# mm2's seven products in one PSUM bank, pages handed out one by one, a fourth block of mm1 by seven products, and a new order of work

## The chip, the cores and the metric

The kernel runs on one core of one Trainium2 chip. The core has five engines that work side by side: TensorE (PE, whose weight loads the profile lists as PEld), VectorE (DVE), ScalarE (ACT), GpSimd (POOL) and SyncE (SP, which issues most of the DMA transfers). The metric is the device time of one execution in microseconds; the figure for the kernel before is the median of three runs, 296.69 us (296.46 to 296.79).

## The reference

Retention attention without softmax, followed by a feed-forward layer:

```python
# q, k, v: [8 batches, 8 heads, 576 positions, 64], float32
scores = matmul(q, k.T) / 8
gamma  = 1 - 2.0 ** (-5 - head)
D      = where(i >= j, gamma ** (i - j), 0)          # per head
attn   = matmul(scores * D, v)
x      = attn.transpose(0, 2, 1, 3).reshape(4608, 512)
h      = x @ w_in                                    # w_in  [512, 2048]
g      = 0.5 * h * (1 + tanh(c * (h + 0.044715 * h**3)))
out    = g @ w_out                                   # w_out [2048, 512], out float32
```

## The kernel before

Attention is done in units of 128 positions of one batch with all eight heads: four full units and a tail of 64 positions for each of eight batches, 40 units in all. Units 0, 2, 5 and 7 are "wide": they hold 256 positions, and the next unit number belongs to them. Within a unit the scores of a half of 64 positions are computed directly and masked; what came before goes through a running state of decayed k-v products, one for each head. q and v are scaled by powers of the decay when they are cast to 16 bits (`cast_q`, `cast_k`, `cast_v`; L424, L439, L269), q and k are transposed by a DMA (`dma_T`, L483) or on PE (`pe_T`, L493, with `copy_T` reading the result), `attend` (L529 to L574) holds the scores, the k-v products and the outputs, `masked` (L691), `state_sum` (L713), `state_decay` (L721) and `state_16` are the steps on DVE, ACT and POOL, and `x_out` (L586 to L599) writes the result into xT.

The feed-forward layer works on nine blocks t of 512 tokens. mm1 (`x @ w_in`) is done in one of two ways. Directly: `mm1` (L757) multiplies 128 rows of w_in for each output and `gelu` (L765) reads the bank. Or by seven products instead of eight (Strassen's scheme in Winograd's form): `sum_w` and `sum_x` prepare sums of blocks of w_in and of x, `product_h` (L957) runs product 1 to 7 of a group of four output columns tiles, `part_h` reads partial results out of PSUM, and `gelu_h` (L975) makes the outputs. Blocks 6, 7 and 8 go this way, the others directly. Products 1, 6, 7 and 4 of `product_h` add onto each other in one bank, and `part_h` copies the state between them.

mm2 (`g @ w_out`) is done directly for block 0 and half of block 8 (`mm2`, L783, and `mm2_cols`, L987), and by seven products for the 15 other pairs of 128-token tiles: `sum_b` and `sum_a` prepare sums of w_out and of g, `product` (L860) runs the products into two PSUM banks, and `assemble` reads them: two copies and five sums for each pair. All sums go through `combine` (L817), all plain copies through `copy_on` (L267 on ACT, L269 on DVE or POOL).

PSUM has eight banks: two for mm1 ("h"), two for mm2 ("o"), two for scores and two for attention outputs. `take` hands out the banks of a pool in turn.

Inputs: `load` (L203 to L221) brings q, k and v of a unit by SP into pages of float32. There are 21 pages, in groups of three: unit u uses group u % 7 up to unit 30, and from unit 31 on one of the first three groups, because pages 9 to 20 then hold the sums for mm1's seven products. The weights are loaded and cast to 16 bits by transfers that POOL issues (L238); w_in comes in eight loads, two for each quarter of its columns, and so does w_out. `busy` (L1003) multiplies the identity on PE without use of the result.

The order of the work on every engine is written out as a list of short steps at the head of the file. A step's letter chooses the function and the numbers its arguments. Each engine runs its own steps in the order of the list and waits by semaphores for what it needs. The letters that matter here: L load, I and J loads of w_in and w_out, q k v casts, D and t transposes, B attend, a o z the state, m mask, x output, N and F mm1 and gelu for half a block's tokens (two tiles of w_in's columns in one bank), s U A l f the seven products of mm1, H T W V those of mm2, S the stores, K busy work.

Of the kernel before, what the change touches and what calls it, by code (L numbers as in the profile page):

```python
# [17 lines left out]
L,0,1 Z,1,v L,0,0 I,2,g L,0,2 L,2,1 L,2,0 Z,2,g q,0 k,0,g I,7,g K,4 K,4 K,4 K,3 K,4 t,0,q,h L,2,2  # L18
L,4,1 c t,0,k,h I,1,g v,0,v X,0 y,0,k,v I,0,g I,3,g a,0,1 y,0,q,v Z,3,v k,2,g K,4 K,1 Y,0,1 t,2,k,o
m,0,1 z,0,1,a I,6,g K,4 Y,0,0 a,1,1 q,2 L,4,0 K,4 t,2,q,h m,0,0 y,2,k,a y,2,q,v I,4,g K,1 R,0 I,5,g  # L20
x,0 Y,2,1 L,5,0 x,1 i,4,v K,3 N,0,2,0 N,0,0,0 g o,1,1 m,2,1 L,5,1 Z,4,g v,2,v F,0,2,0 N,0,12,0 Y,2,0
F,0,0,0 z,1,1,v N,0,4,0 L,5,2 X,2 k,4,g Z,5,v q,4 F,0,12,0 F,0,4,0 t,4,k,o a,2,1 t,4,q,o a,3,1
y,4,q,a N,0,8,0 L,4,2 z,2,1,g L,9,1 N,0,10,0 F,0,8,0 k,5,g m,2,0 L,7,1 R,2 F,0,10,0 y,4,k,v B,4,-1
q,5 x,3 x,2 N,0,14,0 L,7,0 t,5,q,o N,0,0,1 L,7,2 J,1,g F,0,14,0 N,0,6,0 y,5,q,v J,3,g t,5,k,o
F,0,0,1 m,4 j,1,v J,0,g L,9,0 v,5,v J,2,g L,9,2 F,0,6,0 N,0,8,1 L,10,0 N,0,12,1 k,7,v X,5 y,5,k,a
F,0,8,1 z,3,1,g F,0,12,1 v,4,v Y,5,0 a,5,1 m,5,0 a,6,1 N,0,4,1 N,0,6,1 F,0,4,1 q,7 F,0,6,1 t,7,k,o
y,7,k,a N,0,2,1 J,5,g J,4,g N,0,14,1 F,0,2,1 J,6,g L,10,2 B,-1,4 F,0,14,1 x,4 Y,5,1 t,7,q,h y,7,q,a
J,7,g m,5,1 N,0,10,1 v,7,v F,0,10,1 z,5,1,g R,5 x,5 Y,7,0 o,6,1 x,6 O,0,0 O,0,4 q,10,g L,11,1
N,1,4,0 O,0,5 N,1,14,0 F,1,4,0 m,7,0 N,1,2,0 L,12,2 O,0,1 X,7 Y,7,1 F,1,14,0 F,1,2,0 L,15,1 k,9,a
# [12 lines left out]
V,1,0,6,v L,16,0 N,2,10,0 F,2,10,0 k,14,g W,1,1,6 V,1,1,1,v N,2,12,0 z,12,1,v L,16,2 B,13,12 x,12
# [84 lines left out]
def kernel(  # L127
# [38 lines left out]
    def ring(pool, shape, dtype, tag, name, bufs):  # L166
        rings[tag] = n = rings.get(tag, -1) + 1
        return pool.tile(shape, dtype, tag=f"{tag}_{n % bufs}", name=name, bufs=1)

    NR = 7
    pages = const.tile([128, 3 * NR, H, D], F32, name="pages")
    raws = [pages[:, 3 * i : 3 * i + 3] for i in range(NR)]


    LATE = 31

    def raw_of(u):
        return u % NR if u < LATE else (u - LATE) % 3  # L180

    WIDE = (0, 2, NC, NC + 2)

# [888 lines left out]
```

## Time and profile before

| what | value |
|---|---|
| median of three runs | 296.69 us |
| the profiled execution: time, and span of its instructions | 295.65 us, 293.9 us |
| PE busy | 280.3 us (95%), 4064 matmuls |
| DVE, ACT, POOL busy | 216.6, 150.1, 109.6 us |
| DMA | 49.79 MB, mean 169 GB/s |
| granted PE clock | 1.0 in the whole span |

The profile counts an engine as busy from the start of an instruction to its end; matmuls overlap each other, so a busy PE is not a measure of PE at its peak, and the distance between two starts is the better price of one. A line of a group gives the line of the kernel, the engine, the operation, what it writes and reads with the shape, how many there were, the busy time, and the idle time of the engine before them with what ended it. The chain of waits is followed back from the last instruction: at each step to what released it.

### The profile page before, as it was taken

How to read it: one execution, taken by the hardware profiler on the slowest of the kernel's cores; microseconds unless marked ns; L12 is line 12 of the kernel's file. 1: busy time of each engine (PE TensorE's matmuls, PEld its weight loads, DVE VectorE, ACT ScalarE, POOL GpSimd, SP SyncE). 2: the span in 40 equal slices, each digit the busy share in tenths (PEclk: the TensorE clock that was granted, in tenths of full speed). 3: DMA queues.
4: the chain of work that ended last, by engine and by line, in shares of the span. 5: the costliest groups of instructions: out<-in, count | busy, mean ns of one | idle time of the engine just before them, and what ended most of it. 6: DMA issues, size and time to landing. Idle time of an engine off the chain costs nothing.

```text
span 293.9 us, 9639 instructions
## 1 busy us (share of the span) xinstructions
PE 280.3 (95%) x4064; PEld 235.2 (80%) x4064; DVE 216.6 (74%) x447; ACT 150.1 (51%) x289; POOL 109.6 (37%) x168
## 2 busy tenths in 40 slices
PE   3797999999999999999999999999999999999995
PEld 1355886667888888888888888888888788888874
DVE  7686753696865678576678699799889988977740
ACT  2144774334634543554553646546777587665411
POOL 5931910414351084163415544783467123000000
PEclk9999999999999999999999999999999999999999
DMA  7999999997979999989099978899498370002103
GB/s 212 283 236 250 217 220 211 214 179 162 248 142 228 178 186 220 230 206 210 23 235 214 196 166 178 187 204 153 131 195 208 75 205 7 36 8 102 74 25 121
DMA packets 136428, 49.79 MB, mean 169 GB/s; under 512 B 118208, under 2 KB 130880, under 8 KB 136384
## 3 DMA queue, kind: packets, MB, share of 16 engines
q1 hardware_dynamic: 132032, 44.97, 71.3%
q0 software_dynamic: 4352, 4.20, 8.5%
q8 instruction: 32, 0.52, 0.8%
q14 instruction: 12, 0.10, 0.1%
HBM read 36.70 MB, written 9.44 MB: 157 GB/s over the span
## 4 chain that ended last, share of the span: by engine, by line
PE 86%; POOL 5%; DMA 4%; DVE 3%; issue 1%; ACT 0%; POOLq 0%; ACTq 0%
PE bank L860 30%; PE bank L757 27%; PE bank L957 12%; PE bank L783 6%; DMA w_in_sb<-in_moe_w_in_dram 4%; PE sk L553 2%; PE x L529 2%; POOL w_in_sb L238 2%; PE sk L563 1%; PE x L574 1%; PE bank L987 1%; DVE pages L817 1%; POOL wide L269 1%; PE bank L493 1%; PE x L677 1%
## 5 line engine op out<-in xcount | busy, mean ns | idle before, releaser
L757 PE MATMUL bank<-xT,w_in_sb 128*128 128x256 f16 x768 | 94.4, 273 | 2.1 <-DMA w_in_sb<-in_moe_w_in_dram 2.1
L765 ACT ACTIVATE gT<-bank 128x512 f16<-128x512 f32 x96 | 56.7, 598 | 61.5 <-PE bank L757 59.7
L757 PEld LDWEIGHTS <-w_in_sb 128*128 128x128 f16 x768 | 73.8, 98 | 13.7 <-DMA w_in_sb<-in_moe_w_in_dram 2.7
L860 PEld LDWEIGHTS <-ssum 128*128 128x128 f16 x480 | 46.3, 98 | 6.5 <-issue 0.8
L269 POOL CAST sz<-s 64x256 f16<-64x256 f32 x48 | 24.4, 509 | 66.2 <-DVE s L713 45.9
L860 PE MATMUL bank<-tsum,ssum 128*128 128x256 f16 x360 | 46.0, 273 | 0.6 <-DVE ost L817 0.6
L860 PEld LDWEIGHTS <-gT 128*128 128x128 f16 x360 | 34.8, 98 | 4.5 <-issue 0.2
L424 POOL TENSOR_TENSOR qk<-pages,dec 128x512 f16<-128x512 f32 (+1 forms) x20 | 22.2, 1122 | 32.9 <-DMA pages<-in_q_dram 17.2
L860 PE MATMUL bank<-w_out_sb,gT 128*128 128x256 f16 x240 | 31.1, 273 | 0.0
L817 DVE TENSOR_TENSOR ssum<-gT 128x1024 f16<-128x1024 f16 x30 | 23.9, 798 | 3.9 <-ACT gT L765 3.5
L424 POOL TENSOR_TENSOR v<-pages,dec 128x512 f16<-128x512 f32 (+1 forms) x20 | 20.6, 1030 | 15.3 <-DMA pages<-in_v_dram 10.4
L817 DVE TENSOR_TENSOR ost<-u,bank 128x256 f32<-128x256 f32 x45 | 18.1, 416 | 9.5 <-PE bank L860 9.4
L817 DVE TENSOR_TENSOR ssum<-gT,ssum 128x1024 f16<-128x1024 f16 x30 | 23.4, 782 | 0.2
L691 DVE TENSOR_TENSOR ret<-sk,mask 128x512 f16<-128x512 f32 (+1 forms) x32 | 19.8, 618 | 4.3 <-PE sk L563 4.0
L957 PEld LDWEIGHTS <-pages 128*128 128x128 f16 x192 | 18.4, 98 | 2.8 <-issue 0.3
L957 PE MATMUL bank<-pages 128*128 128x256 f16 x144 | 20.3, 273 | 0.3 <-ACT pages L267 0.3
L783 PE MATMUL bank<-w_out_sb,gT 128*128 128x512 f16 x80 | 19.1, 380 | 0.0
L817 DVE TENSOR_TENSOR u<-u,bank 128x256 f32<-128x256 f32 x30 | 12.4, 415 | 8.7 <-PE bank L860 5.0
L713 DVE TENSOR_TENSOR s<-s,sk 128x256 f32<-128x256 f32 x36 | 14.9, 415 | 5.0 <-PE sk L563 4.0
L593 ACT ACTIVATE xT<-x 128x512 f16<-128x512 f32 (+1 forms) x25 | 14.3, 578 | 8.0 <-PE x L574 8.0
L817 DVE TENSOR_TENSOR hc<-hc,bank 128x512 f32<-128x512 f32 x21 | 14.4, 684 | 5.0 <-PE bank L957 2.3
L267 ACT COPY hc<-bank 128x512 f32<-128x512 f32 x19 | 11.1, 585 | 12.5 <-PE bank L957 12.4
(114 smaller groups left out, 425.8 us busy)
## 6 DMA issues: line engine op xcount, KB each, us to landing
out_dram<-ost SPq DMA_DIRECT2D x35, 256.0 KB, 3.4
pages<-in_q_dram SPq DMA_DIRECT2D x32, 256.0 KB, 4.7
pages<-in_v_dram SPq DMA_DIRECT2D x24, 256.0 KB, 4.1
pages<-in_k_dram SPq DMA_DIRECT2D x24, 256.0 KB, 4.3
pages<-in_k_dram SPq DMA_DIRECT2D x4, 512.0 KB, 5.2
pages<-in_v_dram SPq DMA_DIRECT2D x4, 512.0 KB, 6.0
w_in_sb<-in_moe_w_in_dram POOLq DMA_DIRECT2D x8, 256.0 KB, 9.8
w_out_sb<-in_moe_w_out_dram POOLq DMA_DIRECT2D x8, 256.0 KB, 10.6
```

The lines of the kernel that those rows point to most:

```text
L267: nc.scalar.copy(out=o, in_=i)
L269: (nc.vector if eng == "v" else nc.gpsimd).tensor_copy(out=o, in_=i)
L424: eng.tensor_tensor(out=out, in0=s["raw"][:, i, 0:n], in1=dec[:, i // 2, s["j"], 0:n].unsqueeze(2).to_broadcast([128, n, D]), op=ALU.mult,)
L593: nc.scalar.activation(out=xT[:, :, o : o + G * (b - a)].rearrange("c p (h s) -> c p h s", s=G), in_=x[:, a:b].rearrange("c h p s -> c p h ...
L691: nc.vector.tensor_tensor(out=ret[:, :, 0:n], in0=now["two"][:, :, 0, 0:n], in1=mask.unsqueeze(1).unsqueeze(1).to_broadcast([128, 2, n, G] ...
L713: nc.vector.tensor_tensor(out=s32, in0=state[0], in1=kv, op=ALU.add)
L757: nc.tensor.matmul(hps[:, i, :], w_in_sb[:, ct, 128 * (fc + i) : 128 * (fc + i) + 128], xT[:, ct, TB * t % XR + lo : TB * t % XR + hi], st ...
L765: nc.scalar.activation(out=gTs[t][:, fc : fc + TB // (hi - lo), lo:hi], in_=h.pop((t, fc, lo)), func=AF.Gelu_apprx_tanh, bias=0.0, scale=1.0,)
L783: nc.tensor.matmul(ops[t, tcc], gTs[t][:, ft, 128 * tcc : 128 * tcc + 128], w_out_sb[:, ft, :], start=(ft == 0), stop=(ft == NFC - 1),)
L817: (nc.vector if eng == "v" else nc.gpsimd).tensor_tensor(out=out, in0=a, in1=b, op=op)
L860: nc.tensor.matmul(p["ps", bank][:, HN * col : HN * col + HN], a[:, k], b[:, k], start=(k == 0 and i in (1, 6)), stop=(k == HK - 1), skip_ ...
L957: nc.tensor.matmul(p["ps", bank][:, n], w[:, c, 128 * n : 128 * n + 128], x[:, c], start=(n == 0 and c == 0 and i in (1, 2, 5)), stop=(c = ...
```

## The change

Five things change together.

- `product` and `assemble`: products 1, 6, 7 and 4 of a pair now add onto the same half of the first bank, with a copy of the state taken out between them (four copies, one of them straight into the output tile). Products 2, 5 and 3 go into the second bank; three sums read them. The copies can be given to ACT or DVE, the sums are on DVE. A pair had two copies and five sums.
- Pages: `page` and `read` hand out single pages from a list of free ones, the longest free first; a wide load takes two neighbours. From unit 26 on, or once the sums of w_in have begun, only pages 0 to 8 are used.
- mm1 of block 5 is done by seven products too, so four blocks instead of three.
- mm1 of block 0 and block 4 is partly done in other shapes: the new steps M and G do a quarter of the block's tokens for four column tiles in one bank (128 columns for each matmul), or all 512 tokens for one tile.
- The list of steps is made anew: order, and which engine takes each cast and copy. Unit 23 is transposed on PE instead of by DMA, the busy work falls from 36 to 20 matmuls, and the stores and loads stand in other places.

Some further options are added to functions and not used by the list (`sum_a` with 5, `masked` with "h", `state_sum` on POOL).

```diff
-    raws = [pages[:, 3 * i : 3 * i + 3] for i in range(NR)]
-    LATE = 31
-    def raw_of(u):
-        return u % NR if u < LATE else (u - LATE) % 3
+    LATE = 26
+    free = [12, 13, 14] + list(range(12)) + list(range(15, 3 * NR))
+    page_of, sums_on = {}, [False]
+    def page(u, n, width=1):
+        top = 9 if u >= LATE or sums_on[0] else 3 * NR
+        at = {p: i for i, p in enumerate(free) if p < top}
+        p = min(
+            (p for p in at if p + width - 1 in at), key=lambda p: (max(at[p], at[p + width - 1]), p)
+        )
+        for i in range(width):
+            free.remove(p + i)
+        page_of[u, n] = p
+        return p
+    def read(u, n, width=1):
+        free.extend(range(page_of[u, n], page_of[u, n] + width))
...
     def product(t, pr, i):
-        if i in (1, 6):
-            p["ps", 0 if i == 1 else 1] = take("o")
         a, b, bank, col = {
-            1: (blk_a(t, pr, 0, 0), blk_b(0, 0), 0, 0), 2: (blk_a(t, pr, 0, 1), blk_b(1, 0), 0, 0),
-            3: (s[3], blk_b(1, 1), 1, 1), 4: (blk_a(t, pr, 1, 1), tsum[3], 0, 1),
-            5: (s[0], tsum[0], 1, 1), 6: (s[1], tsum[1], 1, 0), 7: (s[2], tsum[2], 0, 1),
+            1: (blk_a(t, pr, 0, 0), blk_b(0, 0), 0, 0), 2: (blk_a(t, pr, 0, 1), blk_b(1, 0), 1, 0),
+            3: (s[3], blk_b(1, 1), 1, 1), 4: (blk_a(t, pr, 1, 1), tsum[3], 0, 0),
+            5: (s[0], tsum[0], 1, 1), 6: (s[1], tsum[1], 0, 0), 7: (s[2], tsum[2], 0, 0),
         }[i]
+        fresh = ("ps", bank) not in p
+        if fresh:
+            p["ps", bank] = take("o")
...
     def assemble(t, pr, i, eng):
-        if i == 0:
-            copy_on(eng, part_of(t, pr, 1), ps(0, 0))
-        elif i == 1:
-            combine(eng, part_of(t, pr, 2), part_of(t, pr, 1), ps(1, 0), ALU.add)
-        elif i == 2:
-            copy_on(eng, block_c(t, pr, 0, 0), ps(0, 0))
-        elif i == 3:
-            combine(eng, part_of(t, pr, 3), part_of(t, pr, 2), ps(0, 1), ALU.add)
-        elif i == 4:
-            combine(eng, block_c(t, pr, 1, 1), part_of(t, pr, 3), ps(1, 1), ALU.add)
-        elif i == 5:
-            combine(eng, block_c(t, pr, 1, 0), part_of(t, pr, 2), ps(0, 1), ALU.add)
-        else:
-            combine(eng, block_c(t, pr, 0, 1), part_of(t, pr, 2), ps(1, 1), ALU.add)
+        if i in (0, 1, 3):
+            copy_on(eng, part_of(t, pr, (1, 2, 0, 3)[i]), ps(0, 0))
+        elif i == 5:
+            copy_on(eng, block_c(t, pr, 1, 0), ps(0, 0))
+        elif i == 2:
+            combine("v", block_c(t, pr, 0, 0), part_of(t, pr, 1), ps(1, 0), ALU.add)
+        elif i == 4:
+            combine("v", block_c(t, pr, 1, 1), part_of(t, pr, 3), ps(1, 1), ALU.add)
+        else:
+            combine("v", block_c(t, pr, 0, 1), part_of(t, pr, 2), ps(1, 1), ALU.add)
```

The head of the list, where the start is decided, before and after:

```diff
-L,0,1 Z,1,v L,0,0 I,2,g L,0,2 L,2,1 L,2,0 Z,2,g q,0 k,0,g I,7,g K,4 K,4 K,4 K,3 K,4 t,0,q,h L,2,2
-L,4,1 c t,0,k,h I,1,g v,0,v X,0 y,0,k,v I,0,g I,3,g a,0,1 y,0,q,v Z,3,v k,2,g K,4 K,1 Y,0,1 t,2,k,o
-m,0,1 z,0,1,a I,6,g K,4 Y,0,0 a,1,1 q,2 L,4,0 K,4 t,2,q,h m,0,0 y,2,k,a y,2,q,v I,4,g K,1 R,0 I,5,g
-x,0 Y,2,1 L,5,0 x,1 i,4,v K,3 N,0,2,0 N,0,0,0 g o,1,1 m,2,1 L,5,1 Z,4,g v,2,v F,0,2,0 N,0,12,0 Y,2,0
+I,1,g g L,4,1 L,2,0 L,0,0 q,2 Z,5,v q,0,g k,4,a L,0,1 L,0,2 k,0,a K,4 K,4 K,4 K,4 K,2 K,1 t,0,q,h
+L,4,0 I,0,g Z,1,v y,0,q,v Z,3,v t,0,k,h t,2,q,h L,2,1 L,2,2 v,0,v y,0,k,a Z,0,g L,5,0 I,2,g Y,0,0
+X,0 m,0,0 a,0,1 q,4 a,1,1 Y,0,1 Z,2,g m,0,1 k,2,a L,5,1 t,2,k,h z,0,1,v t,4,q,o o,1,1 y,2,q,a R,0
+y,2,k,v x,0 Y,2,0 t,4,k,h M,0,0,0 c v,2,v x,1 y,4,k,a m,2,0 y,4,q,v I,3,g K,1 X,2 I,4,g G,0,0,0
+M,0,0,1 L,5,2 z,1,1,g a,2,1 L,4,2 Y,2,1 G,0,0,1 a,3,1 m,2,1 L,7,1 N,0,4,0 L,7,0 N,0,6,0 I,5,g
```

## The prediction

> **What bounds the kernel now.** I read the page first, then the chain of waits in order of time, then who makes TensorE (PE) wait, then busy time by stage, then single instructions.
>
> ```profile
> span 293.9 us, 9639 instructions
> ...
> PE 280.3 (95%) x4064; PEld 235.2 (80%) x4064; DVE 216.6 (74%) x447; ACT 150.1 (51%) x289; POOL 109.6 (37%) x168
> ...
> PE   3797999999999999999999999999999999999995
> ...
> DMA  7999999997979999989099978899498370002103
> ```
>
> PE is full from the fifth slice (29 us) to the last. Before that DMA is full and PE is not. The chain shows which transfer holds PE, and PE's rates:
>
> ```profile
> 14.38 1.38 POOL w_in_sb L238 x2
> 15.76 12.81 DMA w_in_sb<-in_moe_w_in_dram
> 28.61 1.70 PE bank L757 x14
> ...
> 66.33 1.73 PE bank L783 x8
> ...
> 74.68 0.87 PE bank L757 x8
> ...
> 282.12 0.89 PE bank L987 x16
> ```
>
> The last of eight w_in loads lands at 28.57 us and PE runs from there. Matmuls follow each other at 109 ns for 256 columns (0.87 for 8), 216 ns for 512 (1.73 for 8) and 56 ns for 128 (0.89 for 16). PE's waits after 28.6 us are small; from the distances of matmul starts I find 2.6 us in all, nearly all of it in these stages:
>
> ```profile
> PE bank L860 <- DVE ost L817: 0.6, 1, 0.6
> PE bank L957 <- DVE pages L817: 0.4, 1, 0.4
> PE bank L957 <- ACT pages L267: 0.3, 1, 0.3
> ```
>
> ```profile
> 180.00:200.00 20.00, 20.00 (x334) 17.85 (x321) 17.43 (x32) 10.24 (x20) 13.51 (x16) 1.00 1.03 205
> 200.00:220.00 20.00, 20.00 (x346) 17.86 (x345) 17.22 (x37) 14.54 (x29) 9.54 (x14) 1.00 0.76 155
> 220.00:240.00 20.00, 18.95 (x265) 16.45 (x263) 19.32 (x37) 13.57 (x28) 8.45 (x11) 1.00 0.68 159
> ```
>
> The columns are stage, length, then busy us of PE, PEld, VectorE (DVE), ScalarE (ACT) and GpSimd (POOL). PE loses time in the one stage where DVE is 97% busy. So the time is: start, PE's work, DVE where it is dense, and a tail of 3 us.
>
> **The change part by part.** Of the two programs I have the order of instructions on each engine; durations are from the trace.
>
> *PE's work.* mm1's block 5 goes from direct to seven products: product_h has 448 matmuls of 256 columns for 336, +112 x 0.109 = +12.2 us. mm1's direct matmuls were 768 of 256 columns; now 512 of 256 (-27.9 us), 64 of 128 (16 in 0.89: +3.6) and 48 of 512 (+10.4). Together -1.7. Unit 23's transposes move from a DMA to PE: 8 x 0.056 = +0.4. All of it lies on the full PE: **-1.3 us**. mm2's products stay 840.
>
> *The start.* The busy work on PE falls from 36 to 20 matmuls of 512 columns; it stood in waiting time, so it is worth nothing by itself. By 28.61 us PE has done 9.2 us of useful work (36 transposes 2.0, key-value products 0.9, four score products 1.6, one attend 1.0, 34 matmuls of mm1 3.7), so the start costs 19.4. What changes is what is needed first. Before, block 0's first steps take all four quarters of w_in, and all eight loads are issued by 16.5. Now block 0 begins with two quarter-width steps on w_in loads 0 and 1 alone, then needs loads 2 and 3, then 4 and 5. The rows that price this:
>
> ```profile
> L238 POOL DMA_DIRECT2D w_in_sb<-in_moe_w_in_dram x8: 713/724/899, 6.4 to 15.8; - x8
> ...
> DMA to landing us min/median/max: 6.7/10.4/13.3
> ```
>
> I follow POOL's new order by these rows: load 1 at 6.4; then the wide cast of q (the 128x512 one takes 1.04 to 1.20, so 2.1 to 2.4); load 0 at 9.6; load 2 at 10.9; 1.45 of memsets; loads 3 and 4 at 13.6 and 14.3; then a cast that waits for DVE's decayed state, which after two masks of 1.22 I put at 17.9; load 5 at 18.7. Behind that cast stand loads 5, 6 and 7, and for load 5 PE waits. It lands 6.7 later at best (25.4), 10.4 by the median (29.1). PE has then done 10.7 us of useful work (44 transposes 2.5, the same products 2.5, two attends and a first scores step 2.2, 32 matmuls of 128 columns 1.8, 16 of 256 1.7), 1.5 more than before. The gain is 4.7 at best and 1.0 by the median; queueing is lighter here (five loads ahead instead of seven), so I take landing at 26.6: **-3.5 us**. Below that end: if a later load (7, issued near 28.6 behind a cast of q and a gated state) also lands late, the gain is gone and 1 to 2 us with it.
>
> *mm2 gathered in one bank.* A pair had 2 copies and 5 sums out of PSUM and has 4 copies and 3 sums. For 15 pairs 30 sums leave DVE; 48 copies now stand on ACT (30 before), 57 operations on DVE (75): DVE -18 x 0.335 (start to start) = -6.0 us, ACT +18 x 0.37 = +6.7, and ACT is 51% busy. The new wait: products 1, 6, 7 and 4 add onto one region, so each waits for the copy of the state before it, and in PE's queue everything stands behind it. The turnaround is seen in mm1's groups, which already do this:
>
> ```profile
> 253.13 0.58 ACT L267 COPY pages<-bank 128x512 f32<-128x512 f32 x1 [0.69 <-PE bank L957]
> ...
> 253.77 0.60 PE L957 MATMUL bank<-pages 128*128 128x256 f16 x4 [0.29 <-ACT pages L267]
> ```
>
> 0.25 from the last matmul, the copy, 0.06 to the next: 0.89 for 512 columns, 0.68 for mm2's 256 (0.37). In the new list there is at least one product (0.87) between two of a pair that share the region, so this costs 0 if ACT is free; a gelu ahead (0.6) would cost up to 0.4 each time. In mm1's block 8, first group, two steps have only 0.44 between, where before one had: +0.45.
>
> *DVE.* Block 5 brings 12 more copies or sums of 512 (11 of them on DVE, 0.60) and 4 sums of xT (0.44); casts of q, k, v go to POOL and ACT, some state casts come. Added up along the list, DVE has 208 us for 205. But in the stretch from 140 to 240 us of PE work it has 96.1 against 90.6. Before, its densest stretch (20.7 of DVE to 19.7 of PE) is the stage with 19.32 above, and PE lost 1.05. The furthest that DVE's sum runs ahead of PE's rises from 4.1 to 4.5 us at full use of DVE, and from 5.2 to 7.7 if it is used to 93%. So +0.4 to +2.5; I take **+1.5**. Upper end: over the last three blocks before, 54.6 us of DVE work took 62.7; at that ratio the new stretch takes 110, ten more than PE.
>
> What lengthens DVE's sums is in these two rows, the same operation with and without POOL casting beside it:
>
> ```profile
> 226.25 1.42 DVE L817 TENSOR_TENSOR ssum<-gT,ssum 128x1024 f16<-128x1024 f16 x1
> ...
> 231.26 0.68 DVE L817 TENSOR_TENSOR ssum<-gT 128x1024 f16<-128x1024 f16 x1
> ```
>
> The Trainium skill, "SBUF — State Buffer", section "Who interferes with whom", says that a DVE instruction with two SBUF inputs contends with a GpSimd instruction that reads SBUF, and one waits for the whole of the other. The trace agrees (1.42 against 0.68). The change gives POOL 9 more casts of q and v and takes 10 of k and of the state; in the dense stretch POOL has 38 us for 45. By that rule 32 sums that cost 0.13 more on average than alone (0.74 against 0.61, start to start) lose a sixth of it, -0.7 us, an estimate; by the mean row nothing changes, and the sum here keeps that.
>
> *Pages one by one, transposes.* A load finds its page's last reader 8 us of PE work or more behind it (1.5 before), but nine pages must do from unit 26 instead of 31. Five units have their last cast under 4.6 us of PE work before their scores, as five do now, and cast (1.04) plus transposing DMA (3.7) is 4.7; no wait of PE on them shows, since POOL and SP run ahead. Cost 0, with up to 3 if SP no longer runs ahead. I add 0.5 for such odds and ends over all the list.
>
> Sum: -1.3 -3.5 +0.45 +1.5 +0.5 = -2.35. The profiled execution took 295.65 (span 293.9 and 1.7 around it), which gives 293.3; the median of the runs is 1.04 above it: **294.3**.
>
> **The rivals.**
> 1. *Clean:* the stretch 140 to 240 waits no more than now and load 5 lands at 25.4: -1.3 -4.7 +0.5, 291.2. For it: ACT has room and DVE lost 6 us of sums. Against: the 96%.
> 2. *DVE becomes the bound (slower):* in blocks 5 to 8 PE waits for sums. At the ratio 54.6 to 62.7 the stretch costs 10 more, less 2.2 of old waits: 296.7 -4.8 +7.8 +0.5 = 300.2. It ends on the other side once the added waits pass 4.8.
> 3. *The start gains nothing:* load 5 or 7 lands late and PE runs from the same point: 296.7 -1.3 +2.45 = 297.85. For it: three loads stand behind a cast that waits.
> 4. *SP starves on nine pages or late transposes:* +3 on the sum, 297.3.
> 5. *PE cools in the start.* The first busy matmuls run at half pace:
>
> ```profile
> 4.50 5.92 PE L1003 MATMUL bank<-ident 128*128 128x512 f16 x19 [4.50 <-DVE ident L364]
> ```
>
> Eight of the 19 take 0.427, the rest 0.216: cold costs 8 x 0.21 = 1.7. With the later fillers gone PE is patchy from 11 to 18 us and much of what it does there is transposes; should it cool, 294.3 + 1.7 = 296.0. Against: a gap of 1.9 us before the busy matmuls at 13.57 did not cool it. The Trainium skill, "TensorE: Matmul & The Clock Gate", section "What's actually happening", gives half rate after an idle window of about 3.4 us, and its section "Part 4: PE-mode transpose" says that transposes don't count as busy; the gap of 1.9 us agrees with the first, and no run here shows the second.
>
> **How the numbers follow.** A difference under 0.2% (0.6 us) can't be told from none. Chances: forecast 0.36; clean 0.23; cooled 0.08; start without gain 0.13; starved 0.05; DVE bound 0.15. Faster: the first three, 0.67; the starved and start cases lie about the limit, and I give same 0.07; slower 0.26. The range reaches from the clean case with a little over its bounds (290.3) to the DVE case (300.0). The forecast's own range is 292.5 to 296.3.
>
> **What would show it.** The first long run of mm1 on PE near 26 us; 4024 matmuls; DVE near full between 165 and 265 us of the span with PE's waits there on the sums of L850 about 4 us. Wrong would be: PE's waits on copies of mm2's bank in the steady stage, a wait on transposed q and k, a start at 28 us or later, or DVE lagging by more than 5 us.

## The result and the profile after

The kernel after takes 299.52 us in the median of six runs (298.54 to 300.90), the kernel before 296.57 in as many on the same chip (294.80 to 296.98): a ratio of 1.0111 (95% interval 1.0074 to 1.0148). It is slower by 2.95 us, where 2.4 us faster was forecast; the range held it. Here and below, an execution over 1.5% longer than the shortest of its kernel is left out of medians and ratios (one of run 7, one of run 14). The profiled execution after took 298.54, that before 295.65, a difference of 2.89, so the two traces can be set against each other.

The page of the kernel after, parts 1 and 2 (busy time, and the span in 40 slices):

```profile
span 296.8 us, 9578 instructions
...
PE 279.5 (94%) x4024; PEld 230.5 (78%) x4024; DVE 216.1 (73%) x457; ACT 162.9 (55%) x317; POOL 107.7 (36%) x160
...
PE   3759989999999999999999999899999999999995
...
PEclk9978999999999999999999999999999999999999
...
GB/s 151 269 247 246 228 232 201 204 165 191 224 212 205 170 147 190 211 145 227 234 176 137 184 200 168 192 199 236 144 162 211 129 3 71 16 57 38 71 73 107
```

PE has its 4024 matmuls and looks full one slice earlier than before, yet the span is longer. PEclk explains the look: 7 and 8 in the third and fourth slice, where before it was never under 9. And the first slice moved 151 GB/s, where before it was 212.

A busy PE says little, so I use a measure made from the trace. PE's *loss* up to a time is that time less the work that PE has started by then, each matmul at its usual distance to the next (0.216 us for 512 columns, 0.109 for 256, 0.056 for 128, 0.008 to 0.029 for the small ones), busy matmuls at nothing. The prices of the small ones are a choice; another choice moves both rows below alike, so their difference says more than each row.

| up to, us of the span | 28.7 | 36 | 45 | 160 | 190 | 240 | 288 | all useful work |
|---|---|---|---|---|---|---|---|---|
| before | 19.9 | 20.0 | 20.1 | 21.1 | 21.4 | 23.4 | 24.2 | 266.5 |
| after | 19.7 | 19.9 | 21.6 | 22.9 | 24.9 | 26.6 | 28.3 | 265.3 |

The start scatters: three later runs with the very start of the kernel after (6, 7 and 8 below) have lost 20.0, 19.0 and 20.1 us by 28.7 us and 21.9, 20.6 and 21.5 by 45, and run 9, with the start of the kernel before, 20.0 and 20.7. So at 28.7 us the two starts are equal within their scatter, and by 45 us the new one is behind by about 1.

In the two profiled executions the 2.9 us are: PE's work -1.25; the start -0.2; from 28.7 to 45 us +1.65; from 45 to 160 +0.35; from 160 to 190 +1.7; from 190 to the end +0.55; tail +0.1.

**The start.** Busy time by stage, in the order PE, PEld, DVE, ACT, POOL, then the granted clock, the share of DMA and GB/s:

```profile
20.00:24.00 4.00, 4.00 (x71) 3.20 (x70) 2.55 (x3) 2.85 (x5) 1.38 (x3) 0.50 1.17 249
...
36.00:40.00 4.00, 2.62 (x67) 2.24 (x65) 2.11 (x3) 1.87 (x4) 2.36 (x2) 1.00 1.20 216
```

PE is busy without a gap from 20 to 24 us, at a granted clock of 0.50; from 36 to 40 it stands for 1.4. DMA is full in both. The timeline of POOL shows the w_in loads behind casts of the state (start, length, what; idle time ahead of it):

```profile
19.93 0.83 POOL L286 CAST sz<-old 64x256 f16<-64x256 f32 x2 [2.97 <-DVE old L754]
20.71 0.72 POOL L255 DMA_DIRECT2D w_in_sb<-in_moe_w_in_dram  x1
25.18 0.83 POOL L286 CAST sz<-s 64x256 f16<-64x256 f32 x2 [3.76 <-DVE s L746]
...
28.41 0.77 POOL L255 DMA_DIRECT2D w_in_sb<-in_moe_w_in_dram  x1
29.20 1.97 POOL L764 TENSOR_TENSOR sz<-s,gend 64x256 f16<-64x256 f32 x2
31.11 0.76 POOL L255 DMA_DIRECT2D w_in_sb<-in_moe_w_in_dram  x1
```

Load 5 is issued at 20.71 and lands at 28.21; loads 6 and 7 (28.41, 31.11) land at 34.16 and 38.67. Before, the last of the eight landed at 28.56.

But PE does not wait for any of them. Its longest waits from 12 to 46 us (who waits, for whom, us in total, times, longest):

```profile
PE bank L514 <- POOL wide L457: 2.5, 2, 1.3
PE x L686 <- DVE sz L286: 1.3, 1, 1.3
PE x L640 <- DVE wide L457: 1.0, 1, 1.0
...
```

These are casts of the units and the state. No load of w_in stands in this view, where before it was the longest wait of the start (2.1 us, shown at run 15).

**The rest.** PE's four longest waits from 28 us to the end:

```profile
PE bank L514 <- POOL wide L457: 1.2, 1, 1.2
PE bank L1001 <- DVE pages L850: 0.9, 2, 0.6
PE x L550 <- DVE sz L764: 0.7, 1, 0.7
PE bank L904 <- DVE ost L850: 0.5, 1, 0.5
```

The first is at 38 us: the cast of unit 7's q, whose second half landed only at 37.47. The products of mm2 (L904) wait 0.5 us once, for a sum; the gathering in one bank costs nothing that the view shows. The third is at 187 us, and DVE's timeline shows what stood ahead of it, with the same operation 12 us earlier:

```profile
173.31 0.67 DVE L850 TENSOR_TENSOR ssum<-gT 128x1024 f16<-128x1024 f16 x1
...
185.80 1.50 DVE L850 TENSOR_TENSOR ssum<-gT 128x1024 f16<-128x1024 f16 x1
187.22 0.84 DVE L764 TENSOR_TENSOR sz<-s,gend 64x256 f16<-64x256 f32 x2
```

DVE goes from one instruction to the next without a gap, and one sum takes 1.50 where the same operation took 0.67.

### The profile page after: what moved, and what is told of

Read it like the earlier page. It is cut to its first block, busy times and chain, and to the rows that moved or that the text cites. A ratio compares the mean times of both kernels' runs of the same rounds, so it can differ in the third digit from the quotient of the medians.

```text
span 296.8 us, 9578 instructions
## 1 busy us (share of the span) xinstructions
PE 279.5 (94%) x4024; PEld 230.5 (78%) x4024; DVE 216.1 (73%) x457; ACT 162.9 (55%) x317; POOL 107.7 (36%) x160
## 4 chain that ended last, share of the span: by engine, by line
PE 74%; DVE 10%; DMA 4%; SPq 4%; POOL 4%; issue 2%; ACT 1%; POOLq 0%; ACTq 0%; DVEq 0%
PE bank L904 24%; PE bank L790 23%; PE bank L1001 11%; PE bank L816 6%; DMA pages<-in_q_dram 3%; DVE ssum L850 3%; DVE pages L850 2%; SPq L238 2%; PE sk L574 2%; PE x L550 2%; PE bank L514 1%; POOL wide L457 1%; PE bank L1031 1%; PE sk L584 1%; PE x L595 1%
## 5 line engine op out<-in xcount | busy, mean ns | idle before, releaser
L790 PE MATMUL bank<-xT,w_in_sb 128*128 128x256 f16 (+2 forms) x624 | 79.2, 279 | 0.0
L790 PEld LDWEIGHTS <-w_in_sb 128*128 128x128 f16 x624 | 58.6, 100 | 13.0
L798 ACT ACTIVATE gT<-bank 128x512 f16<-128x512 f32 x80 | 47.2, 598 | 36.4 <-PE bank L790 36.3
L904 PEld LDWEIGHTS <-ssum 128*128 128x128 f16 x480 | 46.3, 98 | 6.6 <-issue 0.6
L904 PE MATMUL bank<-tsum,ssum 128*128 128x256 f16 x360 | 46.1, 273 | 0.2 <-DVE ssum L850 0.2
L904 PEld LDWEIGHTS <-gT 128*128 128x128 f16 x360 | 34.8, 98 | 4.8
L904 PE MATMUL bank<-w_out_sb,gT 128*128 128x256 f16 x240 | 31.0, 273 | 0.0
L286 POOL CAST sz<-s 64x256 f16<-64x256 f32 x34 | 17.8, 522 | 36.3 <-DVE s L746 27.8
L441 POOL TENSOR_TENSOR v<-pages,dec 128x512 f16<-128x512 f32 (+1 forms) x25 | 26.0, 1046 | 12.2 <-DMA pages<-in_v_dram 7.3
L1001 PE MATMUL bank<-pages 128*128 128x256 f16 x192 | 28.0, 273 | 0.6 <-DVE pages L850 0.3
L1001 PEld LDWEIGHTS <-pages 128*128 128x128 f16 x256 | 24.3, 97 | 4.3 <-issue 1.0
L722 DVE TENSOR_TENSOR ret<-sk,mask 128x512 f16<-128x512 f32 (+1 forms) x32 | 19.7, 615 | 10.5 <-PE sk L584 9.6
L850 DVE TENSOR_TENSOR ost<-u,bank 128x256 f32<-128x256 f32 x45 | 18.2, 414 | 9.1 <-PE bank L904 5.3
L850 DVE TENSOR_TENSOR ssum<-gT,ssum 128x1024 f16<-128x1024 f16 x30 | 23.5, 783 | 0.2
L850 DVE TENSOR_TENSOR hc<-hc,bank 128x512 f32<-128x512 f32 x29 | 19.7, 680 | 4.7 <-PE bank L1001 2.8
L284 ACT COPY hc<-bank 128x512 f32<-128x512 f32 x26 | 15.2, 584 | 13.8 <-PE bank L1001 13.3
L850 DVE TENSOR_TENSOR ssum<-gT 128x1024 f16<-128x1024 f16 x30 | 22.8, 758 | 0.0
L1001 PEld LDWEIGHTS <-w_in_sb 128*128 128x128 f16 x192 | 18.4, 98 | 4.0 <-DVE pages L850 1.3
L1001 PE MATMUL bank<-xT,w_in_sb 128*128 128x256 f16 x128 | 19.2, 273 | 0.2 <-DVE hc L850 0.2
```

The source lines that it names most:

```text
L284: nc.scalar.copy(out=o, in_=i)
L286: (nc.vector if eng == "v" else nc.gpsimd).tensor_copy(out=o, in_=i)
L441: eng.tensor_tensor(out=out, in0=pages[:, page_of[s["u"], i], 0:n], in1=dec[:, i // 2, s["j"], 0:n].unsqueeze(2).to_broadcast([128, n, D]) ...
L722: nc.vector.tensor_tensor(out=ret[:, :, 0:n], in0=now["two"][:, :, 0, 0:n], in1=mask.unsqueeze(1).unsqueeze(1).to_broadcast([128, 2, n, G] ...
L790: nc.tensor.matmul(hps[:, i, :], w_in_sb[:, ct, 128 * (fc + i) : 128 * (fc + i) + 128], xT[:, ct, TB * t % XR + lo : TB * t % XR + hi], st ...
L798: nc.scalar.activation(out=gTs[t][:, fc : fc + TB // (hi - lo), lo:hi], in_=h.pop((t, fc, lo)), func=AF.Gelu_apprx_tanh, bias=0.0, scale=1.0,)
```

## The experiments

The edits are shown in steps of the list; "..." stands for steps left as they are. "Loss" is the measure above. All times are medians; the ratio is to the kernel before on the same chip. Each trace is of one execution. Intervals of the ratios are some 0.003 wide to either side, so differences among the variants under about 0.004 (1.2 us) are read from the traces, not from the medians.

**1. The start kept warm.**

```diff
-K,1 t,0,q,h ... t,2,q,h ... X,0 ... Y,0,1 ... R,0
+K,1 K,4 K,2 t,0,q,h ... K,3,o t,2,q,h ... K,4,o X,0 ... K,3,o Y,0,1 ... K,6,o R,0
```

> Leaves the kernel after as it is and adds 22 busy matmuls of 512 columns at five places in the start where PE waits (11, 13, 15, 16 and 18 us), so that PE isn't cold when mm1 begins. Clock theory (the granted clock of 0.50 from 18.4 to 25.2 us ate the gain of the start): the clock stays at 1.00, the first steps of mm1 take 0.056 us a matmul of 128 columns instead of 0.11, and PE's loss up to 28.7 us falls from 19.7 us by 1.0 to 1.4, to the point where w_in load 5 (28.2) holds it. Rival (the loads hold the start and the slow clock only fills the wait for them): the clock stays at 1.00 and the loss at 28.7 us moves by less than 0.4. In either case PE's wait at 38 us for unit 7's q, which comes from a load, grows by what was gained, so the total is 298.9 to 299.5 us by both.

Measured: 299.05 us, ratio 1.0089 (1.0064 to 1.0114); granted clock 1.00 in all of the start; the loss at 28.7 us is 19.6 (19.7 after), at 45 us 21.2 (21.6), which is within the scatter, and by 240 us 26.6 as in the kernel after. PE at full clock only waits for something else from 18 us on:

```profile
PE x L641 <- DVE wide L458: 1.5, 1, 1.5
PE bank L515 <- ACT wide L285: 1.1, 1, 1.1
PE bank L791 <- DMA w_in_sb<-in_moe_w_in_dram: 0.5, 1, 0.5
```

The first two are casts that wait for loads of v and k: unit 2's v landed at 23.11 in this execution, at 20.94 in the kernel after, while w_in's loads 2 to 4 landed 2 to 3 us earlier. So PE at full clock met other late loads. The slow clock is real, but taking it away gained nothing that can be told from the scatter.

**2. The w_in loads ahead of the casts on POOL.**

```diff
-z,1,1,g ... I,5,g z,2,1,g ... I,6,g ... I,7,g
+I,5,g z,1,1,g ... I,6,g I,7,g z,2,1,g
```

> The kernel after with the issue of w_in loads 5, 6 and 7 moved ahead of the two casts of the state on POOL behind which they stood. Load theory (the three loads wait behind gated casts, and that is what holds the start and the stretch at 36 to 45 us): load 5 lands near 26.5 instead of 28.2, loads 6 and 7 before 32 instead of 34.2 and 38.7, the loss at 28.7 us falls by 1 us or more, total near 298.3. Clock theory: PE is busy at half clock while the loads come, so nothing changes at 28.7 us (within 0.3), and the total is 299.5 or, since the earlier loads push unit 7's q back in the transfers, up to 1 us more.

Measured: 300.05 us, 1.0130 (1.0109 to 1.0151). Loads 6 and 7 landed at 29.8 and 31.6, as the load theory says, load 5 at 27.7 and not near 26.5. The loss at 28.7 us fell by 0.3 only, at 36 us it was 22.1 instead of 19.9, and the total is that of the clock theory's second case. PE's waits from 26 to 46 us:

```profile
PE x L640 <- DVE wide L457: 1.2, 1, 1.2
PE bank L514 <- DVE wide L286: 0.8, 1, 0.8
```

These are unit 5's casts: its k and v landed at 31.1 and 33.3 now. What one load gained another lost.

**3. Unit 7's transposes later on PE.**

```diff
-t,7,q,o x,5 y,7,q,v x,6 ... M,0,12 ... N,1,8,0 G,0,13 F,1,8,0 ... N,1,10,0 F,1,10,0
+x,5 x,6 ... N,1,8,0 F,1,8,0 N,1,10,0 F,1,10,0 t,7,q,o y,7,q,v M,0,12 ... G,0,13
```

> The kernel after with the transposes of unit 7's q on PE put behind two more steps of mm1 (block 1, tiles 8 to 11, 3.5 us of PE work) that need nothing of unit 7. If the 1.3 us that PE stands at 38 us for these transposes are a loss of the whole execution, the loss at 45 us falls by 1.2 and the total is 298.2. If the steps moved ahead only meet w_in load 5 or 7 or DVE's sums later, the loss is back by 60 us and the total stays at 299.5.

Measured: 300.80 us, 1.0135 (1.0102 to 1.0168), above both expectations; two executions took 298.5 and 298.6, four 300.7 to 301.5, and the trace is of one of the two. In it the loss at 45 us was 20.7, inside the scatter, since the wait only changed its name (PE's waits from 28 to 46 us):

```profile
PE bank L790 <- ACT xT L607: 1.2, 1, 1.2
```

By 240 us the loss was 26.6, that of the kernel after. The first expectation fell; why four executions took 2 us more, the trace can't show.

**4. The three together.** The edits of 1, 2 and 3.

> The three edits of the runs before together: busy matmuls, loads ahead, unit 7's transposes later. Clock theory: 1.3 of the start and 1.2 at 38 us, 297.0. Load theory: the loads give 1 to 2 more on top, as load 5 is then what a warm PE would wait for: 295.5 to 296.5. If neither holds and PE is caught by DVE later anyway, 299 or more.

Measured: 301.56 us, 1.0182 (1.0159 to 1.0205): none of the three. PE's waits at 26 to 46 us were 1.6 for a cast of unit 5, 1.2 for xT and 0.7 for unit 5's v; the loss at 45 us was 23.6. With mm1 ready earlier PE runs into the units' loads sooner.

**5. The old start in the new list.** The steps of the list before up to the first mm2 step of block 0, with their engines, then what is left of the new list.

```diff
-I,1,g g L,4,1 L,2,0 L,0,0 q,2 ... M,0,0,0 ... N,0,8,0 ... M,0,12 G,0,12 ...
+L,0,1 Z,1,v L,0,0 I,2,g L,0,2 ... N,0,10,1 F,0,10,1 ... x,6 | rest of the new list
```

> The steps of the list before up to the first mm2 of block 0 (units 0 to 7, block 0 of mm1 in 256 columns, 36 busy matmuls, the loads in their old order), and behind them the steps of the new list that are then left, in their new order. Theory A (the new start and the stretch to 45 us cost 1.5, and that counts to the end): the loss at 45 us is 20.1 as before instead of 21.6, total 298.0. Theory B (DVE is full from 160 to 260 us of the span and sets the time there, whatever PE brings with it): the loss at 45 us is 20.1, but by 260 us it is 27.0 or more again, total 299.0 to 300. The two runs that gained 0.4 and 0.8 by 45 us and had lost it by 240 us speak for B.

Measured: 299.21 us, 1.0072 (1.0046 to 1.0099), runs from 298.4 to 301.5. The profile fell on the longest of them, in which the last w_in load was issued at 16.64 and landed at 30.67, against 15.76 and 28.56 in the kernel before; the granted clock was 0.50 from 27.5 to 30.9, in mm1; and the loss at 45 us was 22.9. So the trace can't decide between A and B. What it shows is that with one and the same order of loads the last can land 2.1 us later, 0.9 of it by its issue.

**6 and 7. DVE relieved, DVE loaded.** From the end of block 3 to block 6, 15 copies out of PSUM (12 of mm2, 3 of mm1's products) go from DVE to ACT, or 12 copies of mm2 from ACT to DVE:

```diff
-V,4,0,0,v ... V,5,0,5,v ... l,6,2,1,v ... l,7,2,2,v
+V,4,0,0,a ... V,5,0,5,a ... l,6,2,1,a ... l,7,2,2,a
```

```diff
-V,4,0,3,a ... V,4,1,0,a ... V,5,0,0,a
+V,4,0,3,v ... V,4,1,0,v ... V,5,0,0,v
```

> The kernel after with 15 plain copies out of PSUM (11 of mm2, 4 of mm1's products) from block 3 on moved from DVE to ACT: DVE has about 6 us less to do between 160 and 290 us, ACT as much more (it is busy 12 to 14 of 20 us there). Theory B (DVE sets that stretch): PE's loss from 160 to 290 us falls from 5.0 to 3.5 or less, total 298.0 or less. Rival (PE waits there for single late steps, not for DVE's sum of work): the loss stays within 0.5 of 5.0, total 299.2 to 300; if ACT is late with gelu instead, it grows.

> The opposite: 12 copies of mm2 from block 3 on moved from ACT to DVE, DVE 4.0 us more. Theory B: the loss from 160 to 290 us grows by 3 to 4 us, total near 303. Rival: by less than 1, total under 300.5.

Measured: relieved 302.49 us, 1.0182 (1.0140 to 1.0224); loaded 302.14 us, 1.0170 (1.0122 to 1.0218). Both are slower than the kernel after by about 2 us. PE's waits from 160 to 262 us, first with DVE relieved, then with DVE loaded:

```profile
PE bank L904 <- ACT ost L284: 1.1, 1, 1.1
PE bank L1001 <- DVE pages L850: 1.0, 1, 1.0
...
PE bank L1001 <- ACT hc L284: 0.8, 2, 0.5
...
```

```profile
PE bank L1001 <- DVE hc L850: 2.0, 4, 1.1
PE bank L904 <- DVE ost L286: 1.9, 2, 1.6
...
```

Run 7 came out near what theory B said. Run 6 didn't: DVE's busy time from 160 to 260 us fell from 92.5 to 84.7, and the loss there grew. So theory B as I had put it, that DVE's sum of work sets the stretch whatever else changes, falls. But the edit of run 6 gives ACT the work that it takes from DVE (ACT's 65.8 us become 69.0), and part of the new waits is for ACT, so what DVE relieved alone would bring is not shown. What PE waits for in these views are single copies and sums that come late in the order of DVE or of ACT, and either shift makes it worse.

**8. Block 5 direct.**

```diff
-s,5,1 ... A,5,0,1 ... l,5,0,0,a A,5,0,6 ... f,5,0,1
+N,5,0,0 ... N,5,2,0 F,5,0,0 ... F,5,2,0
```

> The kernel after with mm1 of block 5 done directly again (its matmuls in the places of the products, its sums and copies gone): PE has 1.7 us more to do, DVE 9 us less between 165 and 200 us. Theory B: the loss from 160 to 290 us falls from 5.0 to 2 or less, which more than pays for the 1.7: total 298.3 or less. Rival: the loss stays, total 301.

Measured: 300.06 us, 1.0095 (1.0062 to 1.0128), the profiled run 298.99. Its loss from 160 to 190 us is 0.24, where the kernel after loses 1.97. Busy time by stage:

```profile
160.00:180.00 20.00, 20.00 (x324) 17.50 (x322) 15.68 (x29) 10.47 (x23) 11.94 (x14) 1.00 0.86 162
180.00:200.00 20.00, 20.00 (x344) 17.85 (x342) 14.17 (x29) 10.42 (x23) 9.21 (x14) 1.00 0.96 197
```

The same stages of the kernel after:

```profile
160.00:180.00 20.00, 19.69 (x319) 17.07 (x317) 19.24 (x37) 11.96 (x26) 12.05 (x14) 1.00 0.92 163
180.00:200.00 20.00, 19.14 (x331) 16.66 (x329) 18.25 (x37) 13.80 (x29) 8.87 (x14) 1.00 1.12 197
```

Here both DVE and ACT have less to do, and the waits go. So the fourth block by seven products spares PE 1.74 us of work and costs it 1.7 in waits: it is worth nothing in this list. The total lies between the two expectations: the first (1.3 gained in all) was too much, since the later waits stayed.

**9. mm2's new form alone, in the old list.** The kernel before with the new `product` and `assemble`; in each pair the places of the products and sums are kept and filled in an order that the new form allows. In 45 places of the list one product of a shared region follows another, and in 43 of them another product of mm1 or mm2 stands between the two on PE.

```diff
-W,1,0,1 V,1,0,0,a W,1,0,6 W,1,0,2 V,1,0,1,v V,1,0,2,a W,1,0,7 V,1,0,3,v W,1,0,4 W,1,0,5 V,1,0,5,v V,1,0,4,v W,1,0,3 V,1,0,6,v
+W,1,0,1 V,1,0,0,a W,1,0,6 W,1,0,2 V,1,0,1,v V,1,0,2,v W,1,0,7 V,1,0,3,a W,1,0,5 W,1,0,4 V,1,0,5,a V,1,0,4,v W,1,0,3 V,1,0,6,v
```

> One part of the change alone: the kernel before, its list and pages, with mm2's products gathered in one bank and the copies between (45 copies on ACT, 15 on DVE, in the places where the products and sums stood). Theory of the prediction (the new form is free where other PE work lies between two products of a region, and takes 5 us from DVE): 295.0 to 296.7. Rival (every product of a region waits for a copy that stands behind a gelu on ACT): PE's small waits ahead of the products of mm2 add up to 1.5 us or more, 298 or more.

Measured: 302.17 us, 1.0178 (1.0151 to 1.0205). The rival's numbers were right, its mechanism in part. Of PE's waits from 60 us to the end, the longest and the one for copies of the state:

```profile
PE bank L861 <- DVE ssum L817: 2.1, 3, 1.0
...
PE bank L861 <- ACT u L267: 1.0, 2, 0.5
```

One place in PE's and ACT's timelines:

```profile
128.48 0.71 PE L757 MATMUL bank<-xT,w_in_sb 128*128 128x256 f16 x5 [1.02 <-ACT gT L765]
```

```profile
127.56 0.37 ACT L267 COPY u<-bank 128x256 f32<-128x256 f32 x1 [1.85 <-PE bank L861]
127.83 1.09 ACT L765 ACTIVATE gT<-bank 128x512 f16<-128x512 f32 x2
```

ACT stands 1.85 us before the copy of a state of mm2's bank, because its product isn't done; the gelu that mm1 needs stands behind the copy; and PE waits 1.02 for the gelu. A wait that the change adds on one engine is paid by whoever stands behind it there. So 1.0 is for copies directly and 1.0 for a gelu behind one; that the 2.1 for sums of g (`ssum`) and 1.9 for sums of mm1 come of the form too is not shown. In the new list, whose order was made for the form, the products of mm2 wait 0.7 in all.

**10. Another order of the first loads.** Unit 0's loads first, its q cast on DVE, unit 2's on POOL.

```diff
-L,4,1 L,2,0 L,0,0 q,2 Z,5,v q,0,g k,4,a L,0,1 L,0,2 k,0,a
+L,0,0 L,0,1 L,0,2 L,2,0 q,0 Z,5,v k,0,a L,4,1 L,2,1 ... q,2,g k,4,a t,2,q,h
```

> The kernel after with another order of the first loads: unit 0's k, q, v go first, as before, and unit 4's tail, which moves 64 KB a transfer, behind them; unit 0's q is cast on DVE and unit 2's on POOL. Supply theory (what has been moved by a time sets the start; the new list moves 151 GB/s in the first slice where 212 went before): over 190 GB/s in the first slice, the loss at 45 us 1.0 to 1.5 lower, 298.2. Rival (the start is held by the chain of casts, transposes and states and not by what was moved): first transposes 1.5 us earlier, and nothing at 28.7 us, 299.5.

Measured: 299.37 us, 1.0083 (1.0055 to 1.0110). The first slice moved 197 GB/s and the first transposes ran at 10.1 instead of 11.8 us, but PE then stood for 3.4 us behind the copy of unit 0's k on ACT, which I had put behind unit 4's cast, and cooled:

```profile
16.00:20.00 4.00, 2.01 (x68) 1.75 (x69) 2.22 (x5) 2.78 (x4) 1.39 (x3) 0.50 1.19 249
```

The loss at 28.7 us was 22.2. The run doesn't tell the theories apart; 13 is its repair.

**11. That order and block 5 direct.** The edits of 10 and 8.

> That order of the first loads and block 5 direct together. If both of the losses that were found are real and add up, 1.2 less in the start and the stretch from 160 to 190 us without wait for 1.7 of PE work: 298.0. If what is gained early is lost late, 299.5 or more.

Measured: 299.35 us, 1.0078 (1.0050 to 1.0106): near the total of the second expectation, though not by its reason. The start again ran at half clock (loss 21.3 at 28.7 us); from 45 us on the loss grew by 5.4, as in run 8 (5.5), so nothing more was lost late.

**12. 0.5 MB more in the start.**

```diff
-L,2,1
+LL L,2,1
+    def load_again():
+        nc.sync.dma_start(
+            out=spare.rearrange("p (h x) -> p h x", h=H),
+            in_=k[0, :, 0:256, :].rearrange("h (p j) d -> p h (j d)", j=2),
+        )
```

> The kernel after with one more transfer in the start, 512 KB that nothing reads, ahead of unit 2's k. Supply theory: 0.5 MB at 250 GB/s is 2.1 us, the loss at 45 us grows by 1.7 to 2.5 and the total to 301 or more. Rival: the transfers have room, less than 0.5.

Measured: 303.44 us, 1.0210 (1.0170 to 1.0250), the loss at 45 us 26.7 instead of 21.6: 5.1 more, where the supply theory gave 1.7 to 2.5. The chain of waits shows why:

```profile
10.55 12.88 DMA pages<-in_k_dram
...
23.51 1.05 ACT wide L292
```

The load behind the added one, unit 2's k, was issued at 10.55 as in the kernel after (10.27), but landed at 23.43 instead of 16.24, and PE stood 8.1 us for its cast. So the price of a transfer in the start isn't its own time, but what it does to the one that PE needs next.

**13 and 14. Order and clock mended, without and with block 5 direct.** As 10, with unit 4's cast behind the copies on ACT, unit 2's transposes behind unit 0's scores, and 19 busy matmuls in the gaps.

```diff
-q,2,g k,4,a t,2,q,h ... Y,0,0 X,0 ... Y,0,1 ... t,2,k,h ... R,0 ... t,4,k,h
+q,2,g ... K,4,o Y,0,0 K,3,o X,0 ... Y,0,1 ... K,3,o t,2,q,h K,3,o t,2,k,h ... K,6,o R,0 ... k,4,a t,4,k,h
```

> The kernel after with unit 0's loads first, unit 2's transposes behind unit 0's scores, and busy matmuls in the gaps of the start. If supply and clock together ate the gain: the clock stays at 0.9 or more, over 190 GB/s in the first slice, the loss at 28.7 us is 17.5 to 18.8 instead of 19.7, and at 45 us 19.5 to 20.5; total near 298. If what holds the start is that its needed bytes (1.7 MB of unit 0 and 2, the first six w_in loads) take until 28 us at 250 GB/s in any order, the loss at 28.7 us stays within 0.5 of 19.7, total 299 or more.

> The same with block 5 direct. If a gain of the start reaches the end once DVE has room: 1 us under the run before, near 297.5. If not, 299 or more.

Measured: 298.84 us, 1.0076 (1.0048 to 1.0105), and with block 5 direct 298.90 us, 1.0074 (1.0049 to 1.0098). The clock stayed at 1.00, the first slice moved 193 GB/s, and the loss at 28.7 us was 21.1, more than in the kernel after and than either expectation (the trace is of an execution of 299.93). Loads 1 to 4 landed earlier than in the kernel after, but load 5 stood behind POOL's casts again (issued at 22.9, landed at 29.5). The orders of the start that I tried in the new list, warm or cold, have lost 20.6 to 23.6 us by 45 us: none starts clearly sooner than the old start (20.1 in the kernel before, 20.7 in run 9). With block 5 direct the loss from 45 us on is 5.3, as in runs 8 and 11.

**15. The kernel before, with unit 5's loads behind w_in's.** They (1.5 MB) are issued by POOL behind its eight w_in loads, no longer by SP among them; PE's first use of them is at 30.9 us.

```diff
     def load_wide(u, n):
+        eng = nc.gpsimd if u == NC else nc.sync
...
-                nc.sync.dma_start(
+                eng.dma_start(
...
-I,5,g x,0 Y,2,1 L,5,0 ... L,5,1
+I,5,g L,5,0 L,5,1 x,0 Y,2,1
```

> The kernel before, with unit 5's loads (1.5 MB, needed only at 35 us) issued by POOL behind the eight loads of w_in instead of by SP among them. Supply theory: the last w_in load lands 1 to 3 us earlier than 28.6, PE's loss at 32 us is 17.5 to 19 instead of 20.0, total 294 to 295.5. Rival: PE then waits for unit 5's casts at 35 to 40 us by as much, 296.5 or more.

Measured: 295.61 us over 12 runs, ratio 0.9961 (0.9943 to 0.9979): faster than both kernels. The last w_in load landed at 26.75 instead of 28.56, and the loss at 32 us is 18.6 instead of 20.0; it stays about 0.6 to 1.4 lower to the end, though the granted clock was 0.50 from 15.0 to 18.4, where the kernel before had 1.00. PE's waits from 14 to 46 us, of the kernel before and of this one:

```profile
PE bank L757 <- DMA w_in_sb<-in_moe_w_in_dram: 2.1, 2, 1.6
PE sk L636 <- DVE qkT L269: 0.5, 1, 0.5
```

```profile
PE bank L1004 <- DVE qkT L270: 1.9, 1, 1.9
PE sk L637 <- DVE qkT L270: 0.3, 1, 0.3
```

PE no longer waits for w_in; what it still waits for is, but for 0.3, ahead of busy work. The landing and the loss are those of the supply theory; the total is 0.1 above its range.

**16. More out of w_in's way.** Unit 4's v and unit 9's k too.

```diff
-I,5,g L,5,0 L,5,1 ... L,4,2 ... L,9,1 ... L,7,0
+I,5,g L,5,0 L,5,1 L,4,2 ... L,7,0 L,9,1
```

> The kernel before with unit 5's loads behind w_in's, and unit 4's v and unit 9's k (four transfers of 64 KB in the profile's count) put behind them too. If supply still holds the start: the last w_in load lands 0.5 to 1 us earlier than 26.75, the loss at 32 us is 18.0 or less instead of 18.6, total 294.6 to 295.2. If the chain of casts and transposes is next, or unit 4's v is missed: 295.6 or more.

Measured: 296.67 us, 1.0004 (0.9985 to 1.0024): the gain is gone. The chain of waits:

```profile
15.71 13.38 DMA w_in_sb<-in_moe_w_in_dram
...
29.13 1.70 PE bank L759 x14
```

The last w_in load lands at 29.09 again. With unit 4's v on POOL's queue and unit 9's k put behind unit 7's loads, SP came to unit 7's sooner: it issued its k at 12.1 and q at 13.0, beside the w_in loads, instead of 20.5 and later in run 15. The DMA queues from 17 to 26 us (q0 is POOL's, q1 SP's; packets, MB, share of 16 engines), of the kernel before, of run 15, of run 16 and of the kernel after:

```profile
q0 software_dynamic: 1200, 1.16, 75.8%
q1 hardware_dynamic: 1203, 0.93, 41.4%
```

```profile
q0 software_dynamic: 1497, 1.68, 98.1%
q1 hardware_dynamic: 1133, 0.27, 22.8%
```

```profile
q0 software_dynamic: 1297, 1.25, 82.2%
q1 hardware_dynamic: 1296, 0.70, 36.8%
```

```profile
q0 software_dynamic: 969, 0.94, 61.5%
q1 hardware_dynamic: 1956, 1.37, 54.2%
```

In the kernel before and in run 16 the two queues move packet for packet, 1200 against 1203 and 1297 against 1296. In run 15 SP's queue moved nearly as many packets as before (1133), but little in them (0.27 MB instead of 0.93), and w_in's queue moved 1.68 MB instead of 1.16. The Trainium skill, "DMA: Bandwidth & Descriptors", section "Queues, rings and completion order", says that a DMA engine takes turns between the queues that have work, a packet at a time; the rows of the kernel before and of run 16 agree. Those of the kernel after, where SP's queue moved two packets for one of w_in's, don't, and no run here shows why.

## Why the prediction was wrong

**The step that failed** is the start, -3.5 us. Measured: -0.2 at 28.7 us, and with what the late loads did next +1.45 by 45 us. Three of its parts were off. The cast that I put at 17.9 came at 19.93, because the state behind it needs unit 0's v, which landed at 14.23 where before it was 8.64; I had followed POOL's order and not SP's, in which unit 4's parts and unit 2's q now stood ahead of unit 0. So load 5 was issued at 20.7, not 18.7. It took 7.5 us, not the 7.9 that I had chosen between the bounds, and landed at 28.2, not 26.6. And by 28.7 us PE had done 9.0 us of useful work, not 10.7 by 26.6, since the units were as late as w_in. So the wait was wrong too: "for load 5 PE waits", but PE waited for casts of the units and for the state, and for no load of w_in.

Behind these lies one mistake. I priced the start by one transfer, as if "queueing is lighter here": loads that are issued later leave more room. They don't: DMA had a share of 1.08 to 1.17 in every stage from 12 to 28 us in this kernel, so a load that goes ahead makes another late. Runs 2 and 4 show it for the kernel after, run 12 with a transfer added, runs 15 and 16 in both directions for the kernel before. The fall below the lower end, a later load 7 that "also lands late", happened in part: it landed at 38.67, but what PE stood 1.2 us for was unit 7's q (37.47), not the load. That case was given as rival 3 (start without gain, 297.85) with a chance of 0.13. It deserved more, for three loads behind a gated cast were in sight. That the range held the result is luck: its upper end came from the DVE case.

**The cooling**, rival 5, happened too: 0.50 from 18.4 to 25.2 us. Its price was not the 1.7 that I had given. Run 1 took it away and gained no more than the scatter, 0.1 at 28.7 us and 0.4 at 45. The kernel before points the same way: of its 77 executions beside the experiments, 29 had a mean granted clock of 0.992 to 0.994 (3.4 us at 0.50 in 294 give 0.994) and a median of 296.5 us, the other 48 a clock of 0.998 or more and 296.6. Where in the span those 29 were cold is not on record. So "did not cool it", in the argument against, was one execution's luck: runs 9 and 15, with the same gap of 1.9 us, were at 0.50 from 15.0 to 18.4. The Trainium skill, "TensorE: Matmul & The Clock Gate", section "Part 4: PE-mode transpose", says that transposes don't count as PE-busy in the same way. PE's longest gap between 10.6 and 18.4 us was 1.3 us, much of its work there was transposes, and it cooled; with busy matmuls in the gaps (run 1) it did not. That agrees with the rule, though no run separates transposes from the other small matmuls.

**PE's work**, -1.3: measured -1.25.

**DVE and block 8's chain**, +1.5 and +0.45: from 160 us on the loss grew by 5.4 us instead of 3.1, +2.3. The size was nearly right, the reason half. PE's waits on the sums of L850 between 165 and 265 us were put at about 4 us and are 1.1 (0.9 and 0.2). Less work on DVE did not help where ACT got it (run 6); the views show sums and copies that come late one by one on DVE and ACT, among them one at 1.50 instead of 0.67. Run 8 shows that 1.7 of it belongs to block 5's products; block 8's chain was not measured by itself.

**mm2 gathered in one bank**, 0: right in the new list (0.5 and 0.2 us of waits). But the condition that the prediction named, another product between two of a region, is not enough: run 9 meets it in 43 of 45 places and is over 5 us slower than the kernel before. It seems to hang on where the copies and sums stand on ACT and DVE; what in the new list's order makes the form free was not tested.

**Odds and ends**, +0.5: +0.35 from 45 to 160 us.

With the start as measured the terms give -1.25 +1.45 +0.35 +2.3 +0.1 = +2.95; the two profiled executions differ by 2.89, the medians by 2.95. Rival 2 (DVE bound, 300.2) comes near the number, but its +7.8 in the last blocks is not in the trace.

**Open.** Which order of the start would be better in the new list: none was found, so no run takes the lost time back. Why the runs of one kernel scatter by up to 3 us is open; there is one trace of each. Run 5 does not settle what the old start would be worth under the new list. The pages handed out one by one were not tried alone.

## What to carry to other kernels

In a stretch where DMA is full, cost an edit of the loads by all that is needed until PE is full, on every queue, and not by the transfer that PE waits for today: what one load gains another loses, unless one is found that isn't needed there at all (run 15, -1.05 us by sending 1.5 MB behind what PE waits for). Saved PE work by a form that adds copies and sums can be lost to the engines that serve PE in that stage, each by its own order (run 8: 1.74 saved, 1.7 lost). And a wait added to an in-order engine is paid by what stands behind it, as the gelu behind mm2's copy.

## What was not expected of the hardware

- Two queues with large loads moved packet for packet in two kernels (1200 and 1203 in 9 us, 1297 and 1296) and two for one in another (1956 and 969). A load put on the other queue behind the eight of w_in gets its turn later, and the queue it left goes on with the next load at once (run 16).
- One more 0.5 MB transfer delayed the load behind it by 7.2 us, not by 2.
- With the same order of loads the last of w_in landed at 28.56 in the kernel before and at 30.67 in run 5, where it was issued 0.9 us later; the executions of run 5's kernel differ by 3.1 us.
- In the kernel after, PE's clock fell to 0.50 at 18.4 us, though PE was not idle for more than 1.3 us at a time in the 7.8 us before. With the old start it was at 0.50 from 15.0 us in runs 9 and 15 and not in the profiled execution of the kernel before.
